# Three matrix stages on one core: probabilities in two layouts, and a last group whose second product is plain

## The chip, the cores and the metric

The kernel runs on one core of a Trainium2 chip. What counts is the device time of one execution in microseconds, taken as the median of several executions. The kernel before took 1391.87 us (three executions, 1390.69 to 1393.43).

The engines are named as the profile names them: PE (TensorE, matrix products) with PEld for its weight loads, DVE (VectorE), ACT (ScalarE), POOL (GpSimd) and SP (SyncE, which here only issues transfers). SPq is SP's queue of transfers.

## The reference

Three stages run one after the other, all in 32-bit floating point.

```python
# 1. linear attention, for 4 batches x 8 heads, 576 tokens, 64 columns
phi(x) = concat(exp(xw - max|xw|), exp(-(xw - max|xw|)))   # xw = x @ w_phi
num = phi(q) @ (phi(k).T @ v);  den = phi(q) . sum(phi(k)) + 1e-6
x = num / den                                  # 2304 tokens x 512
# 2. feed-forward
h = x @ w_in;  x = maximum(0.01 * h, h) @ w_out            # 512 -> 2048 -> 512
# 3. four experts, each weighted by a normalised probability
p = domain_probs / (domain_probs.sum(-1, keepdims=True) + 1e-9)   # 2304 x 4
for e in range(4):
    out += p[:, e:e+1] * (maximum(x @ w1[e], 0) @ w2[e])   # 512 -> 1024 -> 512
```

## The kernel before

**Precision.** A product of 32-bit numbers is made of three passes: both operands are split into a high part, which TensorE takes at its fast rate, and a low part (value minus high part), and high x high, high x low and low x high are added up in PSUM (`PASS`). So each operand costs a cast (ACT, `ghi` and its like) and a subtraction (DVE or POOL, `glo` and its like).

**Order.** The code issues the work of the first two stages in an order written out as times (`TIMES`, `ORDER`), and a scheduler then fixes the order of every engine's queue by a model of its own. So `load_probs`, which the code calls near the end of the second stage, stands near the start of SP's queue. Each engine works through its queue in order. SP issues all transfers; it uses eight completion semaphores in turn, so that a transfer's issue may also wait until the one eight places ahead has landed.

**Start.** The first batch's attention opens the program: the loads of keys (`kraw`), queries (`qraw`, one per head), values (`v`), then `load_probs`, then the first blocks of the second stage's weights (`r`, 1 MB each, L460). For a query, PE makes the projection (L304), ACT copies it (`pc`, L309), POOL takes the largest absolute value over the partitions (`mb`, L311), DVE subtracts (L316), ACT takes the exponential (`e`, L325), and PE makes the numerator (`nm`, L350). For a key, PE makes `pk` (L219), and `kvp` later (L257).

**Probabilities.** `load_probs` (L140) puts the probabilities into SBUF as `pe[128, 4, 18]`, token 128c+p in partition p and column c, normalises them with four DVE instructions, and writes them to DRAM as `pT[4, 2304]`, one row per expert. In `pe` the tokens that lie next to each other in DRAM lie in different partitions, so that this transfer (L153) writes single elements: 128 x 4 x 18 of them. `pe` weights the first 768 tokens of the third stage; `pT` is read back, spread over all partitions (`pb`, L943), for the other 1536.

**Third stage.** A group k is 256 hidden columns of one expert for 768 tokens; there are 16 per block of tokens and three blocks, so 48 groups in all (n = 48 in `moe2_plan`). For the last two blocks both products of a group are made by a scheme with seven half-size products instead of eight (Strassen-Winograd): `up_product` makes the seven of the first product into PSUM banks x, y and v; `gate` applies the maximum and the probability and gives `b11`, `b12`, `b22`, `b21` (DVE); `gsum` (POOL) makes the combinations `t1` to `t4`; `ghi` and `glo` split them into high and low parts; `down_product` makes the seven of the second product, one group late, each into a PSUM tile `po` (two buffers); `evict` (DVE, L1029) adds each to its sum A[j, 1..7] in SBUF. After a block's last group, `plus` adds the seven sums up into the four quarters of the output, and `store` writes them.

`moe2_plan` writes this order out by hand: `at(t, f)` with B = 14k gives each step a place, and `kept` holds every engine to it. A product of group k stands next to a second product of group k-1:

```python
at(B + 2 * p, up_product, k, p)              # L1056
at(B + 2 * p + 1, down_product, k - 1, p)    # L1099
at(B + 2 * p + 2.0, evict, k - 1, p)         # L1100
```

So the last group's seven second products stand alone at the end (k = n), with the sums and stores of the last block (L1108 to L1116) among and after them. The weights of both products come from DRAM, one block per product (`w_load`, L700), already split and combined; `w2_lo_d` (L764) and `ws_lo` write them there.

Of the kernel before, what the change touches and what calls it, by code (L numbers as in the profile page):

```python
# [86 lines left out]
def body(ctx, tc, kT, qT, vh, w_phi, w_in, w_out, probs, w1, w2, out):  # L87
# [52 lines left out]
    def load_probs():  # L140
        C = NTOK // 128
        nc.sync.dma_start(out=pe, in_=probs)
        psm = cst.tile([128, C], F32, name="psm")
        nc.vector.tensor_reduce(
            out=psm, in_=pe.rearrange("p e c -> p c e"), op=ALU.add, axis=AX.X
        )
        nc.vector.tensor_scalar(out=psm, in0=psm, scalar1=1e-9, scalar2=None, op0=ALU.add)
        nc.vector.reciprocal(psm, psm)
        nc.vector.tensor_tensor(
            out=pe, in0=pe, in1=psm.unsqueeze(1).to_broadcast([128, NE, C]), op=ALU.mult  # L150
        )
        pT.append(drw.tile([NE, NTOK], F32, name="pT"))
        nc.sync.dma_start(out=pT[0].rearrange("e (c p) -> p e c", p=128), in_=pe)  # L153
# [457 lines left out]

    wd = {}
# [87 lines left out]
    def w_load(i, n):  # L700
# [3 lines left out]
        name = (UP, DOWN)[i][p][1]  # L704
# [59 lines left out]
    def w2_lo_d(k, r2):  # L764
        d = wq[k]
        kept(nc.gpsimd.tensor_tensor(out=d[:, 1], in0=r2, in1=d[:, 0].bitcast(F32), op=ALU.subtract))
        t = drw.tile([128, 3, 2, 256], F32, name=f"wp_{k}")
        for z in range(2):
            nc.sync.dma_start(out=t[:, :, z], in_=d[:, z, 1:4].bitcast(F32))
        wd[1, k] = {n: t[:, q] for q, n in enumerate(AOPS[:3])}  # L770
# [226 lines left out]
    def glo(k, name):  # L997
        t = go[k, name]
        kept(nc.gpsimd.tensor_tensor(  # L999
# [30 lines left out]

    def plus(eng, j, a, b):
        kept(eng.tensor_tensor(out=A[j, a], in0=A[j, a], in1=A[j, b], op=ALU.add))

    def store(j, a, i, h):
        t0 = 2 * TH * (j - 1) + TH * h
        r = out[2 * TH * DM :].rearrange("(d s) -> d s", s=NTOK - 2 * TH)
        nc.sync.dma_start(
            out=r[i * 256 : (i + 1) * 256, t0 : t0 + TH].rearrange("(t p) s -> p t s", p=128),
            in_=A[j, a],
        )  # L1040

    def moe2_plan():
# [207 lines left out]
```

## Time and profile before

| | before |
|---|---|
| median of three executions | 1391.87 us |
| profiled execution, its own time | 1391.01 us |
| span of its profile | 1389.2 us |
| PE busy | 1332.2 us (96%) |
| DVE busy | 945.0 us (68%) |
| POOL busy | 653.7 us (47%) |
| ACT busy | 643.3 us (46%) |
| mean granted PE clock | 0.982 of full speed |

The span runs from the first to the last record of the profiled execution; its own time is 1.8 us longer, for what lies around it. Times in the rows are counted from the span's start. The profile names an instruction by its line, what it writes and what it reads (`po<-go,wo`); numbers behind names are left out there, so `b` is any of b11 to b22 and `t` any of t1 to t4. In brackets stands how long the engine was idle ahead of it and what ended that.

### The profile page before, as it was taken

What the parts mean: (1) busy time and instruction counts of PE and PEld (TensorE: products, weight loads), DVE (VectorE), ACT (ScalarE), POOL (GpSimd) and SP (SyncE); (2) the same over time, 40 slices, a digit from 0 to 9 for tenths busy, and PEclk for the clock granted to TensorE, in tenths of its full rate; (3) what the DMA queues carried; (4) which work ended last, traced back from release to release, by engine and by line L of the source; (5) the groups of instructions that cost most, each with busy time, mean ns of one, the idle gap of its engine ahead of it and who ended that gap; (6) DMA issues with size and microseconds to landing.
All of it is one profiled execution on the core that took longest, in us unless ns stands there. A gap on an engine that the chain in (4) does not pass through costs nothing.

```text
span 1389.2 us, 23190 instructions
## 1 busy us (share of the span) xinstructions
PE 1332.2 (96%) x8297; PEld 1284.6 (92%) x8297; DVE 945.0 (68%) x1381; ACT 643.3 (46%) x1228; POOL 653.7 (47%) x534
## 2 busy tenths in 40 slices
PE   5769999999999999998999999999999999999996
PEld 4658999999999999998899899899999999999996
DVE  2559999967777657655766666646666677666667
ACT  3547665766666645533444444343333324323331
POOL 1212101111111105504756666268888879777776
PEclk8899999999999999999999999999999999999998
DMA  9656485433344325726999999998888899787872
GB/s 97 155 174 236 151 282 156 132 113 109 114 129 146 86 70 175 269 61 214 339 301 304 307 360 374 351 331 284 286 286 287 290 370 362 247 262 246 264 242 76
DMA packets 205794, 313.91 MB, mean 226 GB/s; under 512 B 29168, under 2 KB 104560, under 8 KB 205680
## 3 DMA queue, kind: packets, MB, share of 16 engines
q1 hardware_dynamic: 205680, 312.43, 70.6%
q8 instruction: 66, 1.08, 0.3%
q14 instruction: 48, 0.39, 0.1%
HBM read 223.84 MB, written 88.45 MB: 225 GB/s over the span
## 4 chain that ended last, share of the span: by engine, by line
PE 64%; POOL 12%; issue 9%; DMA 6%; DVE 5%; ACT 3%; SPq 0%; POOLq 0%; ACTq 0%; DVEq 0%
PE op L555 12%; PE hp L522 11%; PE po L851 10%; PE po L1013 7%; POOL go L999 7%; POOL t L991 5%; PE kvp L257 4%; PE py L811 4%; PE nm L350 3%; PE py L964 3%; PE px L811 2%; PE pv L811 2%; PE px L964 2%; DMA qraw<-qT 2%; PE pv L964 2%
## 5 line engine op out<-in xcount | busy, mean ns | idle before, releaser
L1029 DVE TENSOR_TENSOR ac<-po,ac 128x768 f32<-128x768 f32 x210 | 200.4, 955 | 128.6 <-PE po L1013 128.5
L1013 PE MATMUL po<-go,wo 128*128 128x384 f32 x1344 | 274.5, 339 | 6.5 <-issue 6.4
L311 POOL PARTITION_ALL_REDUCE mb<-pc x32 | 72.4, 2265 | 379.8 <-ACT pc L309 318.5
L1013 PEld LDWEIGHTS po<-go,wo 128*128 128x128 f32 x1344 | 239.5, 188 | 8.2 <-issue 7.9
L555 PE MATMUL op<-gt,wt 128*128 128x288 f32 x1536 | 220.5, 297 | 2.0 <-DVE gt L126 1.7
L522 PE MATMUL hp<-xh,wt 128*128 128x288 f32 x1024 | 216.5, 298 | 0.0
L555 PEld LDWEIGHTS op<-gt,wt 128*128 128x128 f32 x1536 | 208.2, 188 | 3.8 <-DVE gt L126 1.9
L995 ACT CAST go<-t 128x384 fp32r<-128x384 f32 x128 | 65.8, 514 | 230.7 <-POOL t L991 224.9
L522 PEld LDWEIGHTS hp<-xh,wt 128*128 128x128 f32 x1024 | 167.3, 188 | 1.0 <-ACT wt L125 0.3
L522 PE MATMUL hp<-xl,wt 128*128 128x288 f32 x512 | 151.5, 296 | 0.2 <-DVE xl L126 0.2
L999 POOL TENSOR_TENSOR go<-t,go 128x384 fp32r<-128x384 f32 x128 | 136.8, 1081 | 20.0 <-ACT go L995 20.0
L851 PE MATMUL po<-wd,gh 128*128 128x512 f32 x384 | 130.0, 392 | 0.0
L964 PE MATMUL py<-xo,wo 128*128 128x384 f32 x576 | 117.2, 338 | 0.0
L999 POOL TENSOR_TENSOR go<-b,go 128x384 fp32r<-128x384 f32 x96 | 101.4, 1056 | 9.3 <-ACT go L995 9.3
L964 PEld LDWEIGHTS py<-xo,wo 128*128 128x128 f32 x576 | 102.5, 188 | 0.2
L991 POOL TENSOR_TENSOR t<-b,b 128x384 f32<-128x384 f32 x64 | 65.8, 1028 | 69.8 <-DVE b L984 69.8
L869 DVE SCALAR_TENSOR_TENSOR ob<-po,pe,ob 128x512 f32<-128x512 f32 x90 | 67.3, 748 | 45.4 <-PE po L851 45.4
L522 PEld LDWEIGHTS hp<-xl,wt 128*128 128x128 f32 x512 | 96.1, 188 | 0.8 <-DVE xl L126 0.5
L126 DVE TENSOR_TENSOR wt<-wr,wt 128x512 fp32r<-128x512 f32 x96 | 74.1, 793 | 15.7 <-ACT wt L125 13.9
L851 PEld LDWEIGHTS po<-wd,gh 128*128 128x128 f32 x384 | 72.1, 188 | 13.5
L964 PE MATMUL px<-xo,wo 128*128 128x384 f32 x384 | 77.8, 337 | 0.0
L964 PE MATMUL pv<-xo,wo 128*128 128x384 f32 x384 | 77.7, 337 | 0.0
(144 smaller groups left out, 2637.8 us busy)
## 6 DMA issues: line engine op xcount, KB each, us to landing
wo<-wu SPq DMA_DIRECT2D x224, 256.0 KB, 4.2
wo<-wx SPq DMA_DIRECT2D x128, 256.0 KB, 4.8
wr<-w SPq DMA_DIRECT2D x96, 256.0 KB, 3.0
wo<-wp SPq DMA_DIRECT2D x96, 256.0 KB, 3.5
r<-w SPq DMA_DIRECT2D x32, 512.0 KB, 5.8
wu<-wuh SPq DMA_DIRECT2D x16, 896.0 KB, 5.0
wu<-wul SPq DMA_DIRECT2D x16, 896.0 KB, 5.5
wp<-wd SPq DMA_DIRECT2D x32, 384.0 KB, 5.6
```

The source lines that it names most:

```text
L126: nc.vector.tensor_tensor(out=lo, in0=src, in1=hi.bitcast(F32), op=ALU.subtract)
L311: nc.gpsimd.partition_all_reduce(mb, pc, 128, bass_isa.ReduceOp.absmax)
L522: nc.tensor.matmul(hp[:, n, 0:HS], lhsT=wi[:, a, kk * 128 : (kk + 1) * 128], rhs=x[z][:, kk, n * HS : (n + 1) * HS], start=(kk == 0 and i ...
L555: nc.tensor.matmul(op[:, n, 0:HS], lhsT=wt1[1, C * GF + f][:, a, d * 128 : (d + 1) * 128], rhs=gts[C * GF + f][:, z, n * HS : (n + 1) * HS ...
L811: kept(nc.tensor.matmul(out, lhsT=ws[w][:, AOPS.index(a), kk * 128 : (kk + 1) * 128], rhs=x[z][:, kk], start=first and n == 0, stop=n == 5 ...
L851: kept(nc.tensor.matmul(op.rearrange("p (h m) -> p h m", h=2), lhsT=(gh, gl)[z][:, 2 * f + t, q : q + 128], rhs=d[:, w, f::2], start=n == ...
L869: kept(nc.vector.scalar_tensor_tensor(out=o, in0=op, scalar=ps, in1=o, op0=ALU.mult, op1=ALU.add))
L964: kept(nc.tensor.matmul(out, lhsT=w[:, wz, kk * 128 : (kk + 1) * 128], rhs=x[z][:, kk], start=first and n == 0, stop=n == 5, skip_group_ch ...
L991: kept(nc.gpsimd.tensor_tensor(out=t, in0=gr[k, a], in1=gr[k, b], op=ALU.subtract))
L999: kept(nc.gpsimd.tensor_tensor(out=t[:, 1], in0=gr[k, name], in1=t[:, 0].bitcast(F32), op=ALU.subtract))
L1013: kept(nc.tensor.matmul(t[:, m, 0:TH], lhsT=w[:, wz, m * 128 : (m + 1) * 128], rhs=g[:, z], start=n == 0, stop=n == 2,))
L1029: kept(nc.vector.tensor_tensor(out=A[j, i], in0=src, in1=A[j, i], op=ALU.add))
```

## The change

It has two parts.

**Probabilities.** The host passes them in two layouts. The first is that of before, for `pe`. In the second, partition p holds the tokens 18p to 18p+17 (`pq`). Both are loaded and normalised by the same four DVE instructions, and `pT` is now written from `pq`: for each expert a partition writes 18 neighbouring elements, so the transfer has 128 x 4 runs of 72 bytes.

**Last group (k = n - 1).** Its second product is made of eight plain half-size products instead of seven combined ones (`last_product`). The combinations t1 to t4 and their splits fall away, `glo` of b22 and b21 goes from POOL to DVE, and `glo` of b12 is new on POOL. The weights needed are a11, a12, a21 and a22 alone; a21, which was not in DRAM, is written there with the last group's weights (`w2_lo_d`, k = KA - 1). The sums A[j, 1..7] are added up into the quarters ahead of the last product, four of the seven additions on POOL; then two plain products go into each quarter's PSUM tile (`last_tile`: two banks of px for the first quarter, po for the others), and `final` adds each half tile to its quarter and stores that half.

```diff
     def load_probs():
         C = NTOK // 128
-        nc.sync.dma_start(out=pe, in_=probs)
+        pq = cst.tile([128, NE, C], F32, name="pq")
         psm = cst.tile([128, C], F32, name="psm")
...
+        for q, t in enumerate((pe, pq)):
+            nc.sync.dma_start(out=t, in_=probs[q])
+            nc.vector.tensor_reduce(
+                out=psm, in_=t.rearrange("p e c -> p c e"), op=ALU.add, axis=AX.X
+            )
+            nc.vector.tensor_scalar(out=psm, in0=psm, scalar1=1e-9, scalar2=None, op0=ALU.add)
+            nc.vector.reciprocal(psm, psm)
+            nc.vector.tensor_tensor(
+                out=t, in0=t, in1=psm.unsqueeze(1).to_broadcast([128, NE, C]), op=ALU.mult
+            )
         pT.append(drw.tile([NE, NTOK], F32, name="pT"))
-        nc.sync.dma_start(out=pT[0].rearrange("e (c p) -> p e c", p=128), in_=pe)
+        nc.sync.dma_start(out=pT[0].rearrange("e (p c) -> p e c", c=C), in_=pq)
...
-        name = (UP, DOWN)[i][p][1]
+        name = LAST[p] if i and k == NB * NC2 - 1 else (UP, DOWN)[i][p][1]
...
-        t = drw.tile([128, 3, 2, 256], F32, name=f"wp_{k}")
+        o = 0 if k == KA - 1 else 1
+        t = drw.tile([128, 4 - o, 2, 256], F32, name=f"wp_{k}")
...
+    def last_product(a, b, t, first):
+        k = NB * NC2 - 1
+        w, g = wo[1, k, a], go[k, b]
+        for m in range(2):
+            for n, (wz, z) in enumerate(PASS):
+                kept(nc.tensor.matmul(
+                    t[m],
+                    lhsT=w[:, wz, m * 128 : (m + 1) * 128],
+                    rhs=g[:, z],
+                    start=first and n == 0,
+                    stop=n == 2,
+                    skip_group_check=not first,
+                ))
+
+    def last_tile(one):
+        if one:
+            return [
+                m2["px"].tile([128, 512], F32, tag="x", name="px")[:, 0:TH] for _ in range(2)
+            ]
+        t = m2["po"].tile([128, 2, 512], F32, tag="o", name="po")
+        return [t[:, m, 0:TH] for m in range(2)]
...
+                if k == n - 1:
+                    at(B + 10.1, ghi, k, "b12")
+                    at(B + 10.6, glo, k, "b12")
+                    at(B + 12.2, ghi, k, "b22")
+                    at(B + 12.75, glo, k, "b22", V)
+                    at(B + 13.6, ghi, k, "b21")
+                    at(B + 14.2, glo, k, "b21", V)
+                else:
...
-            if k > KA:
+            if KA < k < n:
                 for p in range(7):
                     at(B + 2 * p + 1, down_product, k - 1, p)
...
-        B = 14 * n
+        B = 14 * (n - 1)
         for t, e, a, b in (
-            (6.2, V, 6, 1), (4.2, V, 3, 5), (2.2, V, 2, 1), (6.4, V, 3, 6), (8.2, V, 7, 6),
-            (8.3, G, 4, 7), (8.4, V, 5, 7),
+            (7.0, G, 6, 1), (9.0, G, 7, 6), (11.0, G, 6, 5), (13.0, G, 5, 7),
+            (12.9, V, 3, 6), (14.3, V, 2, 1), (15.5, V, 4, 7),
         ):
...
+        order = (
+            ("00", "a11", "b11"), ("01", "a11", "b12"), ("01", "a12", "b22"), ("11", "a21", "b12"),
+            ("11", "a22", "b22"), ("00", "a12", "b21"), ("10", "a21", "b11"), ("10", "a22", "b21"),
+        )
...
+        for q, x in enumerate(order):
+            at(B + 14 + q, tail, *x)
+        for t, o, i in ((17, "01", 3), (19, "11", 5), (20, "00", 2), (22, "10", 4)):
+            at(B + t, final, o, i)
```

The orders of all engines differ from those of before in these places alone, but for one 192 KB load of the third block's tokens (L622, `xr2`) that stands four places later on SP.

SP's queue at the start of the program, before (from the loads of `v` to the first weights; what a transfer waits for ahead of its issue in brackets, where DMAHW3 is the completion of an earlier transfer):

```order
L176 DMA v_159<-vh 128x5x192
L142 DMA pe_98<-probs 128x72
L181 DMA qraw_124<-qT 128x576
L181 DMA qraw_126<-qT 128x576 [waits DMAHW0_49]
L169 DMA kraw_130<-kT 128x576 [waits DMAHW1_49]
L181 DMA qraw_133<-qT 128x576 [waits DMAHW2_49]
L153 DMA pT_6482<-pe_98 128x72x1 [waits DMAHW3_49,DVE_49]
L181 DMA qraw_157<-qT 128x576 [waits DMAHW4_49]
L181 DMA qraw_185<-qT 128x576 [waits DMAHW5_49]
L460 DMA r64_210<-w_in 128x2x1024 [waits DMAHW6_49]
L460 DMA r64_212<-w_out 128x2x1024 [waits DMAHW7_49]
```

and now:

```order
L178 DMA v_159<-vh 128x5x192
L145 DMA pe_98<-probs 128x72
L145 DMA pq_6476<-probs 128x72
L183 DMA qraw_124<-qT 128x576 [waits DMAHW0_49]
L183 DMA qraw_126<-qT 128x576 [waits DMAHW1_49]
L171 DMA kraw_130<-kT 128x576 [waits DMAHW2_49]
L183 DMA qraw_133<-qT 128x576 [waits DMAHW3_49]
L155 DMA pT_6488<-pq_6476 128x4x18 [waits DMAHW4_49,DVE_49]
L183 DMA qraw_157<-qT 128x576 [waits DMAHW5_49]
L183 DMA qraw_185<-qT 128x576 [waits DMAHW6_49]
L462 DMA r64_210<-w_in 128x2x1024 [waits DMAHW7_49]
L462 DMA r64_212<-w_out 128x2x1024 [waits DMAHW0_49]
```

The write of `pT` stands behind one more load and ahead of the same `qraw` loads as before; it now waits for the DVE instructions on `pq`.

DVE at the end of the program, from the last group's `b22` on, before (`ac_12643` to `ac_12798` are A[j, 1], 5, 6, 7, 3, 2, 4 in the order 12643, 12671, 12699, 12722, 12745, 12775, 12798; in the queue after, each number is 6 higher):

```order
L984 SCALAR_TENSOR_TENSOR b22_15180<-z_15169,pb_14316 128x384 [waits DVE_49,Pool_49]
L1029 TENSOR_TENSOR ac_12775<-po_15171,ac_12775 128x768 [waits PE_49]
L984 SCALAR_TENSOR_TENSOR b21_15192<-py_7238,pb_14316 128x384 [waits PE_49,Pool_49]
L1029 TENSOR_TENSOR ac_12798<-po_15194,ac_12798 128x768 [waits PE_49]
L1029 TENSOR_TENSOR ac_12643<-po_15209,ac_12643 128x768 [waits PE_49]
L1032 TENSOR_TENSOR ac_12775<-ac_12775,ac_12643 128x768 [waits DVE_49]
L1029 TENSOR_TENSOR ac_12671<-po_15222,ac_12671 128x768 [waits PE_49]
L1032 TENSOR_TENSOR ac_12745<-ac_12745,ac_12671 128x768 [waits DVE_49]
L1029 TENSOR_TENSOR ac_12699<-po_15238,ac_12699 128x768 [waits PE_49]
L1032 TENSOR_TENSOR ac_12699<-ac_12699,ac_12643 128x768 [waits DVE_49]
L1032 TENSOR_TENSOR ac_12745<-ac_12745,ac_12699 128x768 [waits DVE_49]
L1029 TENSOR_TENSOR ac_12722<-po_15249,ac_12722 128x768 [waits PE_49]
```

and now:

```order
L989 SCALAR_TENSOR_TENSOR b22_15182<-z_15172,pb_14322 128x384 [waits DVE_49]
L1034 TENSOR_TENSOR ac_12781<-po_15174,ac_12781 128x768 [waits PE_49]
L1004 TENSOR_TENSOR go_15191<-b22_15182,go_15191 128x384 [waits Activation_49]
L1059 TENSOR_TENSOR ac_12751<-ac_12751,ac_12705 128x768 [waits Pool_49]
L989 SCALAR_TENSOR_TENSOR b21_15195<-py_7244,pb_14322 128x384 [waits PE_49]
L1034 TENSOR_TENSOR ac_12804<-po_15197,ac_12804 128x768 [waits PE_49]
L1004 TENSOR_TENSOR go_15205<-b21_15195,go_15205 128x384 [waits Activation_49]
L1059 TENSOR_TENSOR ac_12781<-ac_12781,ac_12649 128x768
L1059 TENSOR_TENSOR ac_12804<-ac_12804,ac_12728 128x768 [waits DVE_49]
L1165 TENSOR_TENSOR ac_12751<-po_15218,ac_12751 128x384 [waits PE_49]
L1165 TENSOR_TENSOR ac_12751<-po_15218,ac_12751 128x384
L1165 TENSOR_TENSOR ac_12677<-po_15232,ac_12677 128x384 [waits PE_49,Pool_49]
```

The addition of 6 to 3 (`ac_12751<-ac_12751,ac_12705`), which waits for POOL, now stands ahead of `b21`, of the last eviction of the group before (`ac_12804<-po_15197`), and of the low part of b21.

POOL at the end, from the low part of the last b11 on, before:

```order
L999 TENSOR_TENSOR go_15122<-b11_15112,go_15122 128x384 [waits Activation_49]
L991 TENSOR_TENSOR t1_15167<-b12_15158,b11_15112 128x384 [waits DVE_49]
L999 TENSOR_TENSOR go_15178<-t1_15167,go_15178 128x384 [waits PE_49,Activation_49]
L991 TENSOR_TENSOR t2_15190<-b22_15180,t1_15167 128x384 [waits DVE_49]
L991 TENSOR_TENSOR t3_15203<-b22_15180,b12_15158 128x384
L999 TENSOR_TENSOR go_15201<-t2_15190,go_15201 128x384 [waits PE_49,Activation_49]
L999 TENSOR_TENSOR go_15206<-t3_15203,go_15206 128x384 [waits PE_49,Activation_49]
L999 TENSOR_TENSOR go_15216<-b22_15180,go_15216 128x384 [waits PE_49,Activation_49]
L991 TENSOR_TENSOR t4_15231<-b21_15192,t2_15190 128x384 [waits DVE_49]
L999 TENSOR_TENSOR go_15229<-b21_15192,go_15229 128x384 [waits PE_49,Activation_49]
L999 TENSOR_TENSOR go_15235<-t4_15231,go_15235 128x384 [waits Activation_49]
L1032 TENSOR_TENSOR ac_12798<-ac_12798,ac_12722 128x768 [waits DVE_49]
```

and now:

```order
L1004 TENSOR_TENSOR go_15124<-b11_15114,go_15124 128x384 [waits Activation_49]
L1059 TENSOR_TENSOR ac_12705<-ac_12705,ac_12649 128x768 [waits DVE_49]
L1059 TENSOR_TENSOR ac_12728<-ac_12728,ac_12705 128x768 [waits DVE_49,Pool_49]
L1004 TENSOR_TENSOR go_15169<-b12_15160,go_15169 128x384 [waits PE_49,Activation_49]
L1059 TENSOR_TENSOR ac_12705<-ac_12705,ac_12677 128x768 [waits Pool_49]
L1059 TENSOR_TENSOR ac_12677<-ac_12677,ac_12728 128x768 [waits Pool_49]
```

Behind the low part of b11 stood ten instructions of 384 elements and one addition of 768. Now one of 384 (the low part of b12) and four additions of 768 stand there.

## Rows read from the trace of the kernel before

**Rows 1.** Stretches: sum, then busy us of PE, PEld, DVE, ACT, POOL; clock, DMA share, GB/s

```profile
30.00:40.00 10.00, 0.00 (x0) 0.00 (x0) 0.00 (x0) 0.00 (x0) 0.00 (x0) 0.50 1.08 45
40.00:50.00 10.00, 8.20 (x25) 6.43 (x26) 3.87 (x7) 3.15 (x8) 0.00 (x0) 0.68 0.86 303
```

**Rows 2.** Chain of waits at the start: start us, length us, what

```profile
12.31 29.36 DMA qraw<-qT
...
41.80 2.26 PE pq L304 x4
44.06 2.98 PE pk L219 x8
...
56.79 0.97 PE pq L304 x4
57.76 1.73 PE pk L219 x8
```

**Rows 3.** Timeline at the start: start us, length us, instructions, idle before

```profile
11.89 0.38 SPq L153 DMA_DIRECT2D pT<-pe  x1
...
12.24 2.23 PE L304 MATMUL pq<-qraw,wraw 128*128 128x288 f32 x4 [1.99 <-DMA qraw<-qT]
12.31 19.72 SPq L181 DMA_DIRECT2D qraw<-qT  x2
...
14.71 0.75 DVE L316 TENSOR_TENSOR mb<-pc,mb 128x576 f32<-128x576 f32 x1
...
25.33 0.60 PE L219 MATMUL pk<-wraw,kraw 128*128 128x256 f32 x2
...
26.02 1.44 ACT L325 ACTIVATE e<-mb 128x288 f32<-128x288 f32 x4
...
32.07 0.43 SPq L460 DMA_DIRECT2D r<-w_in  x1
...
45.40 1.22 ACT L475 ACTIVATE w<-r 128x512 f32<-128x512 f32 x2 [17.95 <-DMA r<-w_in]
```

**Rows 4.** DMA issues: transfer, count, KB each, median us from issue to landing

```profile
qraw<-qT SPq DMA_DIRECT2D x32, 288.0 KB, 3.6
...
dr<-ds SPq DMA_DIRECT2D x16, 4.5 KB, 1.7
...
pT<-pe SPq DMA_DIRECT2D x1, 36.0 KB, 28.5
...
out<-ac SPq DMA_DIRECT2D x8, 384.0 KB, 3.5
...
out<-ob SPq DMA_DIRECT2D x12, 128.0 KB, 2.2
```

**Rows 5.** Waits of PE from 120 to 1365 us: us in total, times, longest

```profile
PE py L811 <- DVE pz L921: 5.9, 1, 5.9
```

**Rows 6.** Timeline of the tail

```profile
1360.73 1.03 POOL L999 TENSOR_TENSOR go<-b,go 128x384 fp32r<-128x384 f32 x1
...
1366.32 0.56 DVE L984 SCALAR_TENSOR_TENSOR b<-z,pb 128x384 f32<-128x384 f32 x1
...
1366.52 1.22 PE L964 MATMUL py<-xo,wo 128*128 128x384 f32 x6
...
1367.58 4.67 PE L1013 MATMUL po<-go,wo 128*128 128x384 f32 x24
...
1382.55 2.26 PE L1013 MATMUL po<-go,wo 128*128 128x384 f32 x6 [1.56 <-issue]
1384.91 0.96 DVE L1029 TENSOR_TENSOR ac<-po,ac 128x768 f32<-128x768 f32 x1 [1.60 <-PE po L1013]
```

**Rows 7.** Timeline around 909 us, POOL and DVE

```profile
909.66 1.01 POOL L999 TENSOR_TENSOR go<-t,go 128x384 fp32r<-128x384 f32 x1 [0.62 <-ACT go L995]
909.70 1.39 DVE L984 SCALAR_TENSOR_TENSOR b<-z,pb 128x384 f32<-128x384 f32 x1
```

**Rows 8.** Groups of POOL by shape from 860 us on

```profile
L654 POOL TENSOR_TENSOR xt<-xr,xr 128x768 f32<-128x768 f32 x1 | 1.9, 1876 | 0.0
```

More of the change, by code (lines that the diff above doesn't have):

```diff
@@ L766, in w2_lo_d @@
         kept(nc.gpsimd.tensor_tensor(out=d[:, 1], in0=r2, in1=d[:, 0].bitcast(F32), op=ALU.subtract))
-        t = drw.tile([128, 3, 2, 256], F32, name=f"wp_{k}")
+        o = 0 if k == KA - 1 else 1
+        t = drw.tile([128, 4 - o, 2, 256], F32, name=f"wp_{k}")
         for z in range(2):
-            nc.sync.dma_start(out=t[:, :, z], in_=d[:, z, 1:4].bitcast(F32))
-        wd[1, k] = {n: t[:, q] for q, n in enumerate(AOPS[:3])}
+            nc.sync.dma_start(out=t[:, :, z], in_=d[:, z, o:4].bitcast(F32))
+        wd[1, k] = {n: t[:, q] for q, n in enumerate((("a21",) + AOPS[:3])[o:])}
     wsd = {}
@@ L1108, in moe2_plan, with tail, final @@
         j = NB - 1
-        B = 14 * n
+        B = 14 * (n - 1)
         for t, e, a, b in (
-            (6.2, V, 6, 1), (4.2, V, 3, 5), (2.2, V, 2, 1), (6.4, V, 3, 6), (8.2, V, 7, 6),
-            (8.3, G, 4, 7), (8.4, V, 5, 7),
+            (7.0, G, 6, 1), (9.0, G, 7, 6), (11.0, G, 6, 5), (13.0, G, 5, 7),
+            (12.9, V, 3, 6), (14.3, V, 2, 1), (15.5, V, 4, 7),
         ):
             at(B + t, plus, e, j, a, b)
-        for t, a, i, h in ((8.5, 5, 1, 1), (10.1, 3, 0, 1), (12.1, 2, 0, 0), (14.1, 4, 1, 0)):
-            at(B + t, store, j, a, i, h)
+        T = {}
+        order = (
+            ("00", "a11", "b11"), ("01", "a11", "b12"), ("01", "a12", "b22"), ("11", "a21", "b12"),
+            ("11", "a22", "b22"), ("00", "a12", "b21"), ("10", "a21", "b11"), ("10", "a22", "b21"),
+        )
+        def tail(o, a, b):
+            first = o not in T
+            if first:
+                T[o] = last_tile(o == "00")
+            last_product(a, b, T[o], first)
+        def final(o, i):
+            for m in range(2):
+                kept(V.tensor_tensor(out=A[j, i][:, m], in0=T[o][m], in1=A[j, i][:, m], op=ALU.add))
+                store(j, i, int(o[0]), int(o[1]), m)
+        for q, x in enumerate(order):
+            at(B + 14 + q, tail, *x)
+        for t, o, i in ((17, "01", 3), (19, "11", 5), (20, "00", 2), (22, "10", 4)):
+            at(B + t, final, o, i)
         b0 = 14 * KA
@@ L1120, in moe2_plan @@
             at(b0 + 14 * (m // 7) + 2 * (m % 7) + 1.3, w_load, 0, q)
-        for q in range(N_W2E, 7 * (n - KA)):
+        for q in range(N_W2E, 7 * (n - KA) - 3):
             m = q - N_W2
@@ L1230 @@
         "w_out": moe_w_out.reshape(FF1 // 128, 128, DM),
[L1231 removed]
+        "probs": np.stack([
+            moe2_domain_probs.reshape(NTOK // 128, 128, NE).transpose(1, 2, 0),
+            moe2_domain_probs.reshape(128, NTOK // 128, NE).transpose(0, 2, 1),
+        ]),
         "w1": w1.transpose(0, 4, 3, 5, 1, 2, 6).reshape(-1, 128, 4, 256),
```

57 lines of the change are left out of this document (25 added, 32 removed).

## The prediction

> **What bounds the kernel now.** I read the chain of waits first, because it tells which wait ends last. From 120 us on it is PE: in 1245 us its longest wait is 5.9 us [rows 5]. So work taken off other engines there is worth nothing, and time can only come from the two ends. [...] The chain says why: one piece of 29.36 us is a load of a query (`qraw`), issued at 12.31 [rows 2]. The timeline shows what stands ahead of it on SP: the write of `pT` at 11.89, and then SP takes 19.72 us to issue two loads of queries [rows 3]. The list of DMA issues gives the cause: `pT` is 36 KB, yet takes 28.5 us to land, until 40.4; a query of 288 KB takes 3.6 [rows 4]. By the code it is 9216 single elements, 3.1 ns each. The tail I read in the timeline: the last first product starts at 1366.5, the last eviction ends at 1385.87 [rows 6], and the last store ends the span at 1389.2.
>
> **Part 1, the probabilities.** Removed: 28.5 us of small writes. Added: a load of 36 KB, 512 runs of 72 bytes, and four DVE instructions.
>
> When is the new write issued? The order puts the last normalising instruction of `pq` behind the subtraction `mb`, which runs from 14.71 to 15.46 [rows 3]. The added DVE work ahead of and behind it is below 1 us, so I put the issue at 16.6, 4.7 us later than before. The query loads stand behind it on SP and so go at about 17.1 and 17.5, the first weights (1 MB) at 18.
>
> How long does it take? The trace has no transfer of 72-byte runs. From below: at 3.1 ns a run, 512 runs take 1.6 us. From above: the nearest is `dr<-ds`, which by the code is 128 runs of 36 bytes and lands in 1.7 us [rows 4]; four times that is 6.8. I take 2.5, near the row, since from 4.5 KB to 288 KB the time only doubles [rows 4]. Then the query lands at about 17.1 + 3.6 = 20.7, with the upper end at 27.
>
> When does PE need it? Before, PE ran out of work at 25.93, after `pk` [rows 3], and restarted at 41.80 [rows 2]. So a wait of 15.87 us goes. The restart was also at the low clock: `pq` and `pk` took 2.26 + 2.98 us there and 0.97 + 1.73 at 56.79, at the full clock [rows 2]; without the idle time ahead 2.54 us more go. Against this stands the new load on SP: it is ahead of a query for which PE waits 1.99 us at 12.24 [rows 3]; one issue is about 0.45 us there, which PE then loses. This makes 15.87 + 2.54 - 0.45 = 17.96.
>
> What is late next? ACT's casts of the first weights: they waited until 45.40 for a load issued at 32.07 [rows 3]. In the new order ACT reaches them after `e`, at 27.46, so ACT and DVE behind it move by 17.94, about as far as PE. I take 17.5 for the front, as some waits will fit less well. Low end: the weights take as long from issue to use as before, 13.33 us, and are ready at 31.4 instead of 27.9: 14. High end: 18.9, the sum without the added load and half a microsecond of a wait behind. Everything later is issued when an engine before it is done, so the gain travels to the end behind PE.
>
> The load of 192 KB that moves four places on SP, and the 256 KB more written with the last weights, I cost at nothing: PE waits for no transfer in that stretch [rows 5]. If that cover is gone, they are worth one load, some 3 us; I count it in the range.
>
> **Part 2, the last group.** Removed: waits of PE for POOL between the last seven products. Added: an eighth product, at 1.06 us each while PE runs on (1366.52 to 1367.58 in [rows 6]). If nothing waited, PE would end at 1368.65 + 8 x 1.06 = 1377.1 instead of 1384.8. But DVE and POOL have to keep up, and I follow them on before's clock.
>
> POOL: the low part of b11 ends at 1361.76 [rows 6]; then two additions of 768 elements at 1.88 us [rows 8] to 1365.6, the low part of b12 to 1366.6. DVE's gate of b22, at 1366.32 [rows 6], has both its operands in SBUF. What that does stands in rows from elsewhere: at 909.70 the same instruction began 0.04 us after one on POOL and took 1.39 us instead of 0.56, so it ran when POOL's 1.01 us were over [rows 7]. [...] By such turns, on the rows: gate of b22 to 1367.2, POOL's third addition (6 += 5) to 1369.1, low part of b22 on DVE to 1369.65, POOL's fourth to 1371.55, and only then DVE's 3 += 6, to 1372.5. Queued behind that waiting instruction on DVE are the gate of b21 (0.56, to 1373.1), the last eviction of the group before (0.96 as in [rows 6], to 1374.1), the low part of b21 (to 1374.7), two additions (0.96 each, to 1376.6) and eight half evictions of 0.58: 1381.25.
>
> PE meanwhile: three products to 1371.75, then the fourth needs the `po` tile that the eviction frees at 1374.1, a wait of 2.3 us; the seventh needs the tile of the first `final`, done at 1377.8; PE ends at 1379.95, ahead of DVE. So DVE sets the end: 1385.87 - 1381.25 = 4.6 us. The last store is half as large: from the end of the last eviction to the end of the span were 3.3 us; between 2.2 us (128 KB) and 3.5 (384 KB) [rows 4] I take 0.4 less. The tail is worth 5.0 us. High end, no turns at all: the same chain ends at 1378.2, 8.1. Low end 2: PE's clock could fall in its wait; the last product of before took 2.26 us instead of 1.06 after its wait [rows 6], and three products at that length end some 3 us later.
>
> **The sum.** 17.5 + 5.0 = 22.5 us. The profiled execution took 1391.01 us, 0.86 less than the median. 1391.01 - 22.5 = 1368.5, on the median's side 1369.4: I say 1369.
>
> **Rivals.** (a) The weights bind at the front. For: both 1 MB loads stand behind the write and the queries, and took 13.33 us from issue to use. Against: 8 us of that were the rest of the write of `pT`, and the DMA engines are free after it now. Gain 14 + 5 = 19: 1372.4. (b) DVE and POOL don't take turns. For: most DVE instructions beside POOL keep their 0.56 us; against: the rows from 909 us [rows 7]. 17.5 + 8.1: 1365.8. (c) The change doesn't do what it says: the write goes by elements, runs or not. Then it is issued 4.7 us later and PE restarts at 46.4, 4.6 us later; the tail gives 5.0 back: 1391.5. Against: `dr<-ds` has 1152 elements and takes 1.7 us, which is within 3.1 ns an element (3.6 us) and so half an argument; but its runs are nine elements long, and it lands in less than half of that. (d) Slower: a short run costs far more than an element. One mechanism, at the write of `pT`: PE's restart is the landing plus 1.3 us (40.4 to 41.7 before), so with the tail's 5.0 the kernel gets slower from a landing of 16.6 + 29 us on; at twice the old 28.5 us PE restarts at 74.9, 33 us late, less 5: 1420. [...] Against (d) is the 1.7 us again: 128 runs of 36 bytes would have to cost as much.
>
> **How the numbers follow.** My forecast 0.66, its own range 1364 to 1375 (front 14 to 18.9, tail 2 to 8.1, taken together less than at their ends); (a) 0.12, (b) 0.14, (c) 0.03, (d) 0.02, and 0.03 for what I don't see. A measurement of this kernel tells a change from none at about 0.2%, 2.8 us. Faster 0.95, same 0.03, slower 0.02. The range is 1364 to 1377: it holds (a) and (b), leaves out (c) and (d), and has room above for the 3 us of the moved loads.
>
> **What would show it.** Right: `pT` lands in under 7 us; PE goes from `pk` to the next `pq` near 26 with no wait over 1 us, and the first `nm` starts near 29; the wait of ACT for `r<-w_in` shrinks from 17.95 to almost nothing; in the tail DVE's 3 += 6 waits for POOL, PE waits once for about 2 us at its fourth plain product, and eight half evictions end the program. Wrong: `pT` still takes tens of microseconds, or the gap at the start comes back at the first weights or later in the first batch, or the last eviction ends less than 2 us earlier behind the last first product than before.

## The result, and the profile after

The changed kernel took **1355.07 us** (median of four executions, 1353.94 to 1357.85) beside 1392.03 of before on the same chip: a ratio of 0.9737, 95% interval 0.9719 to 0.9756. That is 37 us less, where 22.5 were forecast, and below the low end of the range. Measured once more, later, it was 1354.51 beside 1388.37 (ratio 0.975, 0.9722 to 0.9778). The profiled execution took 1355.73 us, its span 1354.0.

| | before | after |
|---|---|---|
| span of the profile | 1389.2 us | 1354.0 us |
| PE busy | 1332.2 us (96%) | 1318.8 us (97%) |
| DVE busy | 945.0 us | 937.4 us |
| POOL busy | 653.7 us | 647.0 us |
| mean granted PE clock | 0.982 | 0.994 |

**The start.** The stretches that answer to [rows 1]:

```profile
30.00:40.00 10.00, 10.00 (x66) 9.01 (x65) 6.38 (x11) 7.96 (x20) 4.18 (x2) 1.00 0.55 159
40.00:50.00 10.00, 9.68 (x62) 8.11 (x60) 7.43 (x11) 8.00 (x18) 4.28 (x2) 1.00 0.22 48
```

All engines work where all stood still, at the full clock (1.00 in both stretches; 0.50 and 0.68 before). The DMA issues that answer to [rows 4]:

```profile
qraw<-qT SPq DMA_DIRECT2D x32, 288.0 KB, 3.9
...
dr<-ds SPq DMA_DIRECT2D x16, 4.5 KB, 1.5
...
pT<-pq SPq DMA_DIRECT2D x1, 36.0 KB, 2.8
```

The write of `pT` lands in 2.8 us instead of 28.5. The timeline that answers to [rows 2, 3] follows. The name `pq` stands for two tiles there: in `pT<-pq` it is the second layout of the probabilities, in `pq<-qraw,wraw` the projection of a query in PSUM.

```profile
12.03 1.24 PE L306 MATMUL pq<-qraw,wraw 128*128 128x288 f32 x4 [1.68 <-DMA qraw<-qT]
...
13.58 1.21 PE L306 MATMUL pq<-qraw,wraw 128*128 128x288 f32 x4 [0.31 <-DMA qraw<-qT]
...
14.63 1.89 PE L221 MATMUL pk<-wraw,kraw 128*128 128x256 f32 x8
...
16.51 0.38 SPq L155 DMA_DIRECT2D pT<-pq  x1
...
16.93 0.98 SPq L183 DMA_DIRECT2D qraw<-qT  x2
...
21.79 0.60 PE L221 MATMUL pk<-wraw,kraw 128*128 128x256 f32 x2
...
22.22 1.13 PE L306 MATMUL pq<-qraw,wraw 128*128 128x288 f32 x4
...
23.19 1.89 PE L221 MATMUL pk<-wraw,kraw 128*128 128x256 f32 x8
...
24.92 1.13 PE L352 MATMUL nm<-e,kv 128*128 128x288 f32 x4
25.32 1.23 ACT L477 ACTIVATE w<-r 128x512 f32<-128x512 f32 x2 [1.41 <-DMA r<-w_in]
...
27.14 3.18 PE L352 MATMUL nm<-e,kv 128*128 128x288 f32 x12 [1.08 <-ACT kt L244]
```

SP issues two queries in 0.98 us where it took 19.72, and PE goes from `pk` at 21.79 to the next `pq` at 22.22, where before it went from 25.33 to 41.80.

**The third stage.** PE has no gaps there, before or after, yet it is faster now. Each engine's work from 1000 to 1100 us (columns as in [rows 1]), of before:

```profile
1000.00:1100.00 100.00, 100.00 (x569) 100.00 (x568) 65.85 (x88) 35.39 (x73) 86.64 (x81) 1.00 0.86 288
```

and after:

```profile
1000.00:1100.00 100.00, 100.00 (x578) 100.00 (x577) 66.96 (x89) 35.55 (x73) 86.23 (x83) 1.00 0.89 301
```

In 100 us at the full clock PE did 569 matmuls before and does 578 now. PE's queue is the same there, so it can also be read by the same instructions: from the 5900th matmul to the 7000th a matmul took 176.2 ns before and takes 173.6 now.

**The tail**, as a timeline that answers to [rows 6]:

```profile
1337.59 0.82 DVE L989 SCALAR_TENSOR_TENSOR b<-z,pb 128x384 f32<-128x384 f32 x1
1337.84 1.20 PE L969 MATMUL py<-xo,wo 128*128 128x384 f32 x6
1337.95 4.29 POOL L1059 TENSOR_TENSOR ac<-ac 128x768 f32<-128x768 f32 x2
...
1339.20 1.34 DVE L1004 TENSOR_TENSOR go<-b,go 128x384 fp32r<-128x384 f32 x1
...
1340.46 2.60 DVE L1059 TENSOR_TENSOR ac<-ac 128x768 f32<-128x768 f32 x1
...
1343.45 0.94 DVE L1034 TENSOR_TENSOR ac<-po,ac 128x768 f32<-128x768 f32 x1
...
1344.32 0.54 DVE L1004 TENSOR_TENSOR go<-b,go 128x384 fp32r<-128x384 f32 x1
1344.45 2.36 PE L1041 MATMUL po<-go,wo 128*128 128x384 f32 x12 [1.24 <-DVE ac L1034]
1344.78 1.81 DVE L1059 TENSOR_TENSOR ac<-ac 128x768 f32<-128x768 f32 x2
1346.52 1.94 DVE L1165 TENSOR_TENSOR ac<-po,ac 128x384 f32<-128x384 f32 x4
...
1349.97 1.02 DVE L1165 TENSOR_TENSOR ac<-po,ac 128x384 f32<-128x384 f32 x2 [0.58 <-PE po L1041]
```

DVE's 3 += 6 (1340.46) takes 2.60 us beside POOL's two additions; the eviction behind it comes at 1343.45, and PE waits 1.24 us for it at its fourth plain product.

**Where the 35.2 us of span came from.** PE's queue has the same order in both kernels up to the last group, so the starts of the same matmul can be set against each other. Before minus after was

| at PE's matmul number | before | after | difference |
|---|---|---|---|
| 100 (first batch) | 49.8 us | 29.2 us | 20.6 us |
| 4500 (third stage, early) | 679.5 us | 658.0 us | 21.5 us |
| 8200 (last group) | 1359.0 us | 1330.4 us | 28.6 us |
| end of the span | 1389.2 us | 1354.0 us | 35.2 us |

So the start gave 20.6 us, the third stage 7.1, the tail 6.6; 0.9 between the 100th and the 4500th I don't put down to the change: in the same stretch e1_pad32 (below) gained 3.4 us and e3_tail lost 2.8, though their code there is that of before. The table is of one profiled execution of each kernel; by the medians the gain is 37.0 us the first time and 33.9 the second.

### The profile page after: what moved, and what is told of

The parts are those of the page before. It is cut to its first block, busy times and chain, and to the rows that moved or that the text cites. A ratio compares the mean times of both kernels' runs of the same rounds, so it can differ in the third digit from the quotient of the medians.

```text
span 1354.0 us, 23193 instructions
## 1 busy us (share of the span) xinstructions
PE 1318.8 (97%) x8303; PEld 1275.6 (94%) x8303; DVE 937.4 (69%) x1385; ACT 642.1 (47%) x1225; POOL 647.0 (48%) x528
## 3 DMA queue, kind: packets, MB, share of 16 engines
q8 instruction: 66, 1.08, 0.3%
## 4 chain that ended last, share of the span: by engine, by line
PE 85%; DVE 7%; DMA 4%; issue 2%; ACT 1%; POOL 1%; SPq 0%; DVEq 0%; ACTq 0%; POOLq 0%
PE po L1018 16%; PE op L557 12%; PE hp L524 11%; PE po L856 10%; PE py L969 7%; PE px L969 5%; PE pv L969 5%; PE kvp L259 4%; PE py L816 4%; PE nm L352 3%; PE px L816 2%; PE pv L816 2%; PE pk L221 1%; DMA r<-w_out 1%; DVE wt L126 1%
## 5 line engine op out<-in xcount | busy, mean ns | idle before, releaser
L1034 DVE TENSOR_TENSOR ac<-po,ac 128x768 f32<-128x768 f32 x203 | 193.9, 955 | 123.4 <-PE po L1018 123.3
L1018 PE MATMUL po<-go,wo 128*128 128x384 f32 x1302 | 260.9, 336 | 0.0
L1018 PEld LDWEIGHTS po<-go,wo 128*128 128x128 f32 x1302 | 228.7, 188 | 0.4 <-ACT ac L1032 0.2
L1004 POOL TENSOR_TENSOR go<-t,go 128x384 fp32r<-128x384 f32 x124 | 132.5, 1080 | 19.4 <-ACT go L1000 19.4
L1004 POOL TENSOR_TENSOR go<-b,go 128x384 fp32r<-128x384 f32 x95 | 98.0, 1032 | 9.2 <-ACT go L1000 9.2
L126 DVE TENSOR_TENSOR wt<-wr,wt 128x512 fp32r<-128x512 f32 x96 | 74.0, 791 | 16.1 <-ACT wt L125 15.9
L538 DVE TENSOR_TENSOR g<-hp,hs 128x576 f32<-128x576 f32 x64 | 48.0, 750 | 43.0 <-ACT hs L536 42.8
```

The lines of the kernel that those rows point to most:

```text
L126: nc.vector.tensor_tensor(out=lo, in0=src, in1=hi.bitcast(F32), op=ALU.subtract)
L1004: kept(eng.tensor_tensor(out=t[:, 1], in0=gr[k, name], in1=t[:, 0].bitcast(F32), op=ALU.subtract))
L1018: kept(nc.tensor.matmul(t[:, m, 0:TH], lhsT=w[:, wz, m * 128 : (m + 1) * 128], rhs=g[:, z], start=n == 0, stop=n == 2,))
L1034: kept(nc.vector.tensor_tensor(out=A[j, i], in0=src, in1=A[j, i], op=ALU.add))
```

## The experiments

**1. Shift the tiles alone.** The new tile `pq` holds 288 bytes a partition, and every tile allocated from the left behind it lies 288 bytes further on: the weights `wo`, part of the tokens `xo`, the sums `ac`. Those from the right (`go`, `b`, the rest of `xo`) stay. e1_pad32 is before with an unused tile.

```diff
+    pad = cst.tile([128, 8], F32, name="pad")
```

> The kernel before with one unused tile of 32 bytes per partition behind `pe`, so that all tiles allocated from the left move up by 32 bytes and nothing else changes: the third stage's weights and its streamed operands then start at the same place within 64 bytes, as in the kernel after (before: weights at multiples of 64, most streamed tiles 32 above). Theory A (the pace of PE in the third stage hangs on where its two operands lie relative to each other): 100 products' passes of blocks 2 and 3 take 17.35 us instead of 17.61, and the kernel gets about 6.9 us faster, near 1385. Theory B (the pace changed because of the other transfers or the removed stall, or differs from run to run): no change, 1392.

Measured: 1383.64 us beside 1389.39 of before, ratio 0.9953 (0.9938 to 0.9969): 5.8 us less, where 6.9 were expected. `pT` still took 28.1 us; from 1000 to 1100 us PE did 578 matmuls (PE's columns alone):

```profile
1000.00:1100.00 100.00, 100.00 (x578) 1.00 0.87 290
```

So 32 unused bytes give the pace of after, with nothing else of the change.

**2. Each part alone.** e2_probs is part 1 alone, with that unused tile too (so the left tiles lie 320 bytes on); e3_tail is part 2 alone, with no tile moved.

> The kernel before with the change's first part alone (second layout of the probabilities, write of `pT` in runs of 72 bytes), and 32 bytes per partition of padding, so that tiles allocated from the left move by 320 bytes and keep their place within 64. The front alone: PE reaches the second `pk` of eight near 37 us instead of 57.8, that is 20.6 us earlier, and the stage of the feed-forward 21.6 earlier; 1370.4 if theory A holds, since the third stage's pace stays at 17.61 us per 100. Theory B (the pace changed with the transfers): 6.9 more, 1363.5. The prediction's own working for the front was 17.5: 1374.5. Whether the clock falls near 12 us, as it did before, is open: with it the front is worth about 3 us less.

Measured: 1362.83 us, ratio 0.9817 (0.9801 to 0.9834). The start gave 20.6 us at the 100th matmul, as in after; the pace was the fast one. So the time is the one that theory B named; theory A had the pace slow here. But e1_pad32, which has the transfers and the start of before, is fast too, and B doesn't allow that.

> The kernel before with the change's second part alone (last group's second product plain). No tile moves. Tail worth 6.5 us by the two traces, 5.0 by the prediction: 1385.5 or 1387. Start as before, with PE's wait of 15.9 us near 26 to 42 us. Theory A: pace 17.61 us per 100 in the third stage; theory B (the pace hangs on the tail's part or its transfers): 17.35, 1378.6.

Measured: 1385.37 us, ratio 0.9969 (0.9957 to 0.9981). From the 8200th matmul to the end it took 23.4 us, where before took 30.2; 570 matmuls from 1000 to 1100 us, the pace of before. Its profile lost 2.8 us ahead of the 4500th matmul, where its code is that of before. The product of the two ratios, 0.979 (0.976 to 0.982 from the ends of their intervals), lies above after's first measurement (0.9737, up to 0.9756) and meets its repeat (0.975, up to 0.9778). In us the two parts alone make 26.6 + 4.0 = 30.6 by the medians, after's repeat 33.9; where the rest lies these runs don't show.

**3. After with the unused tile**, to turn the pace back.

```diff
+    pad = cst.tile([128, 8], F32, name="pad")
```

> The kernel after with 32 bytes per partition of padding, so that tiles allocated from the left lie 320 bytes above those of before: weights and streamed operands of the third stage are apart within 64 bytes again, as before. Nothing else changes. Theory A: the third stage's pace falls back to 17.61 us per 100, 6.9 us lost: 1362. Theory B: no change, 1355.

Measured: 1356.46 us, ratio 0.9769 (0.9754 to 0.9783), span 1353.9, pace of e2_probs, no loss. The theory as I had put it fell: whether weights and streamed operands start at the same place within 64 bytes does not decide the pace. So I looked for the rule.

**4. Which places are slow.** Before with 128 and with 256 bytes on the left, and with 32 on the right end.

```diff
+    pad = cst.tile([128, 32], F32, name="pad")        # e5_pad128
+    pad = cst.tile([128, 64], F32, name="pad")        # e6_pad256
+    rp = ec(tc.tile_pool(name="rp", bufs=1, side="right"))   # e7_rpad
+    rpad = rp.tile([128, 8], F32, name="rpad")
```

> The kernel before with an unused tile of 128 bytes a partition, so that the tiles allocated from the left lie 128 bytes further on. So far PE took 176.1 ns a matmul from 4500 to 5500 of its matmuls with no shift, and 173.6 with shifts of 32, 288 and 320 bytes. Theory P, the place of the left tiles counts by its remainder to 128 or less (a shift by 64 is known to differ from none through 320, if 256 is a period): 176.1 ns again, time as before. Rival Q, before lies in one bad place of a longer period or of none: 173.6 ns, some 7 us less than before.

> The kernel before with an unused tile of 256 bytes a partition. If the place counts by its remainder to 256 or to less: 176.1 ns a matmul in the third stage's later blocks, time as before. If there is no such period, or what counts is the distance to single other tiles: 173.6 ns, some 7 us less than before.

> The kernel before with an unused tile of 32 bytes a partition at the right end, so that the tiles allocated from the right lie 32 bytes lower and those from the left stay. Theory D, what counts is how operands from the left (weights) and from the right (the gated values, half of the tokens) lie to each other: 173.6 ns a matmul, some 7 us less, as with the 32 bytes on the left. Theory L, only the place of the left tiles counts: 176.1 ns, time as before.

(The text on e5_pad128 names the wrong matmuls: 176.1 and 173.6 ns belong to those from about 5900 on.) Measured, one execution each beside 1386.37 of before: 1385.92, 1389.61 and 1381.76 us. The times alone can't show 7 us: nine executions of before in a later measurement went from 1385.37 to 1395.51, and e5_pad128, though its pace was fast, was only 0.45 us below before. So I go by the pace of the same matmuls (table below): fast with 128 bytes, slow with 256, fast with 32 on the right. A shift of either side helps, and 256 bytes is none.

**5. Shift both sides alike**, and give after the place of before.

```diff
+    pad = cst.tile([128, 8], F32, name="pad")         # e13_both, on before
+    rpad = rp.tile([128, 56], F32, name="rpad")
+    pad = cst.tile([128, 56], F32, name="pad")        # e14_after_224, on after
```

> The kernel before with an unused tile of 32 bytes on the left and one of 224 on the right: the left tiles lie 32 bytes higher, the right ones 224 lower, which is 32 higher by the remainder to 256. Each of the two shifts was a good place by itself so far (32 left: 173.6 ns a matmul; for the right, 32 lower: 173.6). Theory D, what counts is the distance between left and right tiles by its remainder to 256, which is that of before again: 176.1 to 176.2 ns a matmul, no gain. Rival L, before has a bad place on either side and leaving it on one side is enough: 173.6 ns, some 7 us less than before.

> The kernel after with an unused tile of 224 bytes a partition, so that its left tiles lie 512 bytes beyond those of before: the placement of before by the remainder to 256, all else as after. Theory, 7 us of the gain were placement alone: 176.1 ns a matmul in the third stage's later blocks, 6.5 to 7.5 us more than after in the span, 1360 to 1364, and 0.980 to 0.982 of before. Rival, the faster pace belongs to something else in the change: 173.6 ns, time of after.

Measured: e13_both 1390.91 us (one execution) beside 1389.86 of before, and the slow pace again. Alone, the 32 bytes on the left had been fast (of the right side, 32 bytes had been tried alone, not 224); together the two leave the distance as it was, by the remainder to 256. e14_after_224 took 1362.34 us (1360.05 to 1362.97), ratio 0.9796 (0.9772 to 0.9821), span 1361.2, 7.2 more than after. Its row:

```profile
1000.00:1100.00 100.00, 100.00 (x569) 100.00 (x568) 66.35 (x88) 34.94 (x72) 84.31 (x81) 1.00 0.88 292
```

With the start addresses of the built programs (before: `wo` at 6528, `go` at 141792; 128 and 224 by the remainder to 256), ten of the kernels fall into four classes:

| kernel | left shifted by | right shifted by | right minus left, mod 256 | matmuls, 1000 to 1100 us | ns a matmul, 5900th to 7000th |
|---|---|---|---|---|---|
| before | 0 | 0 | 96 | 569 | 176.2 |
| e6_pad256 | 256 | 0 | 96 | 569 | 176.2 |
| e13_both | 32 | -224 | 96 | 569 | 176.2 |
| e14_after_224 | 512 | 0 | 96 | 569 | 176.2 |
| after | 288 | 0 | 64 | 578 | 173.6 |
| e1_pad32 | 32 | 0 | 64 | 578 | 173.6 |
| e7_rpad | 0 | -32 | 64 | 578 | 173.6 |
| e2_probs, e4_after_pad | 320 | 0 | 32 | 578 | 173.5 |
| e5_pad128 | 128 | 0 | 224 | 577 | 174.0 |

Theory D holds in all of them: the distance between left and right tiles decides, by its remainder to 256. In the second stage, whose operands `xh`, `gt` and `wt` all lie on the left, no shift changed the pace: from the 2000th matmul to the 3000th it was 128.7 to 128.9 ns a matmul in every kernel.

**6. Undo the runs alone.** e8_elements is after, with `pT` written from `pe` in single elements again, at the same place of SP's queue.

```diff
-        nc.sync.dma_start(out=pT[0].rearrange("e (p c) -> p e c", c=C), in_=pq)
+        nc.sync.dma_start(out=pT[0].rearrange("e (c p) -> p e c", p=128), in_=pe)
```

> The kernel after with the write of pT in single elements again (from pe, at the same place of SP's queue); the second layout is still loaded and normalised. Theory, the single elements are the cause at the start: the write takes about 28 us, PE waits 15 to 20 us for a query and restarts between 41 and 47, the time is 1371 to 1378; the tail and the pace of the third stage stay as after. Rival, what moved the start was the order on SP and the later issue: PE waits for nothing over 2 us, time 1355 to 1358.

Measured (one execution): 1374.49 us, span 1372.7, 18.7 more than after. Its timeline at the start:

```profile
11.35 0.38 SPq L155 DMA_DIRECT2D pT<-pe  x1
11.77 18.84 SPq L183 DMA_DIRECT2D qraw<-qT  x2
...
40.99 2.26 PE L306 MATMUL pq<-qraw,wraw 128*128 128x288 f32 x4 [14.58 <-DMA qraw<-qT]
```

The old wait is back with the elements, though the second load and its instructions are still there. At the 100th matmul 19.2 of the 20.6 us were gone. One thing else moved: this write doesn't wait for `pq` and was issued at 11.35, not at 16.51, so that this run alone doesn't rule out that the later issue helped. The next one does.

**7. Another length of run.** e10_pairs is after with a layout of pairs, so that `pT` is written in 4608 runs of 8 bytes.

```diff
-            moe2_domain_probs.reshape(128, NTOK // 128, NE).transpose(0, 2, 1),
+            moe2_domain_probs.reshape(NTOK // 256, 128, 2, NE).transpose(1, 3, 0, 2).reshape(128, NE, NTOK // 128),
...
+            out=pT[0].rearrange("e (c p r) -> p e c r", p=128, r=2),
```

> The kernel after with tokens 256c + 2p and 256c + 2p + 1 in partition p, so that pT is written in 4608 runs of 8 bytes in place of 512 of 72. Theory, each run costs about the same whatever its length (9216 took 28.5 us, 512 took 2.8, so 2.95 ns a run and 1.3 us): lands in about 15 us, PE waits some 5 to 9 us for a query, time 1360 to 1365. Rival, elements count, unless runs are long: 28 us, time 1371 to 1378. Rival, the cost is per partition or per row of the destination: under 5 us, time 1354 to 1358.

Measured (one execution): 1368.07 us; its DMA row, its issue and PE's wait:

```profile
pT<-pq SPq DMA_DIRECT2D x1, 36.0 KB, 16.8
```

```profile
16.48 0.38 SPq L155 DMA_DIRECT2D pT<-pq  x1
...
33.60 2.26 PE L309 MATMUL pq<-qraw,wraw 128*128 128x288 f32 x4 [11.25 <-DMA qraw<-qT]
```

The landing fits a price per run (16.8 us where 15 were expected; elements would be 28, rows under 5). The wait and the time were above what I had expected, 11.25 us for 5 to 9: I had let PE come to it later than it does. The write was issued at 16.48, as in after, and PE's wait is back: the number of runs makes it, not the time of the issue.

**8. Another queue.** e9_actq is before with the element-wise write issued by ACT.

```diff
-        nc.sync.dma_start(out=pT[0].rearrange("e (c p) -> p e c", p=128), in_=pe)
+        nc.scalar.dma_start(out=pT[0].rearrange("e (c p) -> p e c", p=128), in_=pe)
```

> The kernel before with the write of pT issued by ACT, so that it goes through a queue of its own; it still writes 9216 single elements. Theory Q, the queries stand behind the elements in SP's queue: they now land in about 4 us, PE's wait of 15 us and more at the start goes, and the time is 1369 to 1374. Rival E, the DMA engines themselves are taken up by the elements, whichever queue they came from: queries still land after 20 us or more, PE restarts near 41, time 1388 to 1393.

Measured (one execution): 1377.98 us beside 1388.37 of before: between the two. The queries that SP had issued ahead of the write (it was issued at 12.50) came in time, and the 100th matmul started at 28.7. But what was issued while the elements ran was late. A stretch (columns as in [rows 1]), a transfer and a wait of SP's queue:

```profile
20.00:28.00 8.00, 8.00 (x50) 7.06 (x49) 4.76 (x10) 5.99 (x13) 0.36 (x1) 1.00 1.92 7
```

```profile
v<-vh SPq DMA_DIRECT2D x1, 480.0 KB, 16.5
```

```profile
SPq L367 <- DMA pT<-pe: 11.3, 1, 11.3
```

7 GB/s, though both queues had work (SP issued `v` at 22.87 and a query at 23.34); 480 KB took 16.5 us; and SP waited 11.3 us for `pT` itself. At the 500th matmul 12.0 of the 21.1 us were left. So the elements take up the DMA engines, from whichever queue they come, and a second queue helps only what is already ahead.

**9. A better order at the end.** e11_plus is after with the addition that made PE wait moved behind the eviction. e12_after is after once more, beside it.

```diff
-            (12.9, V, 3, 6), (14.3, V, 2, 1), (15.5, V, 4, 7),
+            (14.25, V, 3, 6), (14.3, V, 2, 1), (15.5, V, 4, 7),
```

> The kernel after with DVE's addition of 6 to 3 at the end moved behind the last eviction of the group before and the low part of b21. Theory, PE's wait of 1.24 us at the fourth plain product comes from that addition, behind which the eviction is queued: the wait goes, and the end comes 0.5 to 1.3 us earlier behind the last first product. Rival, DVE sets the end whatever its order, and the additions are only put off: the end stays within 0.3 us. The time differs from after's by under 0.1% in either case, so the trace decides.

> The kernel after once more, beside before and the others on one chip: 35 to 38 us less than before if its parts add up with nothing left out (22 at the start, 7 of the third stage's pace, 6.5 of the tail); 30 or less if the first measurement was high by chance.

Measured: e11_plus 1354.31 us, ratio 0.9743 (0.9716 to 0.977); e12_after 1354.51, ratio 0.975 (0.9722 to 0.9778). That is 33.9 us less than before, short of the 35 to 38 that I had expected and more than the 30 of its rival: after came out as the first time, before 3.7 us lower. The tail of e11_plus:

```profile
1337.98 1.20 PE L969 MATMUL py<-xo,wo 128*128 128x384 f32 x6
...
1341.09 0.94 DVE L1034 TENSOR_TENSOR ac<-po,ac 128x768 f32<-128x768 f32 x1
1341.11 4.32 PE L1041 MATMUL po<-go,wo 128*128 128x384 f32 x24
...
1342.76 2.68 DVE L1059 TENSOR_TENSOR ac<-ac 128x768 f32<-128x768 f32 x3
...
1348.81 1.02 DVE L1165 TENSOR_TENSOR ac<-po,ac 128x384 f32<-128x384 f32 x2 [0.58 <-PE po L1041]
```

Four products run through without the wait, and from the start of the last first product the span has 14.8 us left (1337.98 to 1352.80), where e12_after has 16.1. The theory is right by the trace; in the time the 1.3 us can't be told from none.

## Why the prediction was wrong, step by step

The direction and both mechanisms were right; the forecast of 22.5 us was 12.7 short of the 35.2 of the span. By its own terms, that is 3.1 at the start, 7.1 in the third stage, 1.6 in the tail, and the 0.9 that I leave open. Without the 7.1 the time would have been near the low end of the range: e14_after_224, the whole change but for them, took 27.5 us less than the before beside it, and 1391.87 - 27.5 is 1364.4 (its own median was 1362.34).

**The write** (right). Issue put at 16.6, landing taken as 2.5; measured 16.51 and 2.8. Rivals (c) and (d) fall with that. 36 KB in runs of 72, 8 and 4 bytes took 2.8 us (after), 16.8 (e10_pairs) and 28.5 (before), so here the time went with their number.

**"PE ran out of work at 25.93"** (wrong, the step that failed at the start). I took this time over into the changed kernel. But in the profile of before PE reached it late, because its clock was low for a while (granted 0.50 from 14 to 18 us, 1.00 from 20 to 28). The stretch from 12 to 20 us, of before:

```profile
12.00:20.00 8.00, 7.08 (x17) 4.96 (x18) 3.45 (x5) 4.90 (x10) 4.04 (x2) 0.57 1.00 13
```

and after:

```profile
12.00:20.00 8.00, 7.66 (x44) 6.50 (x45) 7.74 (x13) 5.78 (x11) 4.28 (x2) 1.00 0.22 36
```

The first two `pq` and the `pk` behind them took 2.23 + 2.26 + 2.87 us at a granted clock of 0.57, and 1.24 + 1.21 + 1.89 at the full clock after. Before, that cost nothing, since PE then waited for the query whatever it had lost; with the wait gone it would have counted. Six other kernels with the start of before show the wait without that stretch, at a granted clock of 1.00 from 12 to 20 us: 18.27 us in e1_pad32, 17.21 in e3_tail, 20.21 in e5_pad128, 18.25 in e6_pad256, 17.20 in e7_rpad, 20.16 in e13_both, all with a restart between 41.1 and 42.7. So the 15.87 from which I worked was the wait of one execution, and it happened to be a short one. After, PE is at the next `pq` at 22.22, not at 25.93 + 0.45. The 0.45 didn't come either: PE's wait at 12.03 was 1.68, before 1.99. So the wait was worth 41.80 - 22.22 = 19.6; the low clock behind it (0.50 from 42 to 46 us; 2.54 forecast) was worth 2.2, since `pq` and `pk` there took 1.13 + 1.89 after and 2.26 + 2.98 before; and about 1.2 were given back, mostly where PE waits 1.08 us for ACT's `kt` at 27.14. That is the trace of rival (a): ACT still waits 1.41 us for the weights, where I had said almost nothing. 19.6 + 2.2 - 1.2 = 20.6, against 17.5 and a high end of 18.9.

**"time can only come from the two ends"** (wrong, the largest term: 7.1 us, put at nothing). I had looked for transfers and waits in the third stage, and there was nothing. What I left out is that a new tile moves others. I had treated PE's duration of a matmul as a constant of the kernel; it was not, and 7 us came from `pq` lying where it does. e14_after_224 shows it: all of the change, the place of before, 7.2 us of span lost; e1_pad32 is the counterpart. Nothing in the change aimed at it: that before lay in the one slow place of the four seen here was luck. No row of before would have told this, since a profile of one placement shows one pace; with the built programs' addresses I could have said that the term was unknown, and put it in the range with either sign.

**The tail** (right in mechanism, 5.0 for 6.6). The turns of DVE and POOL came as I had followed them; rival (b), without turns, is refuted by the low part of b22 (1.34 us on DVE at 1339.20; 0.54 for that of b21, with POOL done) and by the 2.60 us of 3 += 6. Both have all their operands in SBUF; the eviction at 1338.34, with one operand in PSUM, took 0.94 us beside POOL's third addition, no longer than the one at 1343.45, when POOL was done. POOL's four additions took 1.86 to 2.17 us, the last two, beside these instructions, 2.17 and 2.04. Every piece was a little too long. Counted from the start of the last first product (1366.52 before, 1337.84 after), 3 += 6 was forecast to end at 6.0 us and ended at 5.2, the eviction at 7.6 and 6.6, the last half eviction at 14.7 and 13.15. Half evictions took 0.49 where they came in a row of four, not 0.58; PE waited 1.24, not 2.3, and its clock stayed at 1.00 (1337 to 1353 us).

**What would show it.** `pT` below 7 us: yes. No wait of PE over 1 us near 26: 1.08 us at 27.14. First `nm` near 29: at 24.92, for the reason above. ACT's wait almost nothing: 1.41. The tail: as said.

## What to carry to other kernels

Count a small transfer by its runs, and look at what stands behind it in every queue: 36 KB in 9216 pieces held up loads of eight times the size for 20 us in before, and another queue did not free them (e9_actq: 7 GB/s from 20 to 28 us). A term taken from a wait needs the time at which the engine would be ready without it, and a stretch at a low clock ahead of the wait (here 0.57 from 12 to 20 us) spoils that reading. Where a change adds or resizes a tile, compare the pace of an unbroken stretch of PE before and after; if it moved, unused tiles tell whether placement did it. One pad may hit a place as fast or as slow as the old one (32 more bytes on after and 256 on before changed nothing), so take one that puts the tiles back where they were, or several.

## What the runs showed of the hardware

**PE's pace went with where its operands lie.** With PE busy without a gap, at the full clock, the same 384-column matmuls took 176.2 ns each at a distance of 96 between left and right tiles (mod 256), 173.6 at 64, 173.5 at 32, 174.0 at 224: 1.3 to 1.5% between the slowest and the others, repeated to 0.1 ns in every kernel of a class. What lies behind it was not tried, nor were other distances. But the traces can be split by where a matmul's streamed operand lies (its weights always lie on the left), by the addresses of the built programs. From the 5900th to the 8190th matmul, ns from one start to the next:

| right minus left, mod 256 | streamed `go` (right) | streamed `xo` (right) | streamed `xo` (left) |
|---|---|---|---|
| 96 (four kernels) | 176.2 to 176.4 | 176.8 to 177.0 | 173.8 to 174.0 |
| 64 (three) | 173.2 to 173.3 | 173.2 to 173.3 | 175.8 to 176.0 |
| 32 (two) | 173.4 | 173.3 | 174.7 |
| 224 (one) | 174.1 | 173.4 | 175.6 |

So the loss at 96 falls on the matmuls that stream from the right. Those that stream from the left have their own two operands at the same distance in every kernel, and yet they change too, the other way and by up to 2 ns. So the two operands of a single matmul are not the whole account; what is stays open.

**Runs.** 512, 4608 and 9216 pieces of the same 36 KB landed in 2.8 us (after), 16.8 (e10_pairs) and 28.5 (before): 3.4 ns a piece over the first step, 2.5 over the second. The 9216 single elements took 27.4 to 30.2 us in the nine kernels that wrote them, from SP's queue or from ACT's.

**Split operands.** In after, two products of 288 columns of operands that were not split took 0.97 us (`pq`, four instructions, from 22.22 to the next start at 23.19). In the second stage one of the three passes over split operands, 288 columns too, took 128.8 ns.
